# Pooling attention, then a soft mixture of experts, on one core: phi loaded from another DMA queue

## The chip, the cores and the metric

The kernel runs on one core of one Trainium2 chip. The metric is the device time of one execution in microseconds. The time before is the median of three runs.

## The reference

Queries, keys and values have 8 batches, 8 heads, 576 positions and 64 dimensions. Keys and values are averaged over groups of 8 positions, which leaves 72 of them; each query attends to these 72. The result, 4608 tokens of 512, goes through a soft mixture of 8 experts with 4 slots each.

```python
k_p = k.reshape(B, H, Sp, pool, D).mean(axis=3)
v_p = v.reshape(B, H, Sp, pool, D).mean(axis=3)
scores = scale * np.matmul(q, k_p.transpose(0, 1, 3, 2))
attn = softmax(scores)                       # over the 72 pooled keys
x = np.matmul(attn, v_p)  ->  (4608, 512)
...
logits = x @ phi                             # 4608 x 32 slots
d = softmax of logits over the tokens
slot_input = d.T @ x                         # 32 x 512
h = np.maximum(slot_input[e] @ w1[e], 0.0)   # per expert, 512 -> 1024
slot_out[e] = h @ w2[e]                      # 1024 -> 512
c = softmax of logits over the slots
out = c @ slot_out
```

The array in question is phi: 512 x 32 in fp32, 64 KB. The inputs q, k and v are 9.4 MB each, w1 and w2 16.8 MB each, the output is 9.4 MB.

## The kernel before

**Stages.** The batches are worked on in four pairs. For each pair the kernel loads keys, queries and values as bf16 (the DMA casts them from fp32), pools keys and values with matmuls against a pooling matrix (`pool_stage`, L232 and L236), turns means and queries (L248, L264), computes scores (L309), exponentials on ScalarE (L311), and the products with the pooled values (L331), which VectorE divides by their sums (L336, L342). The preparation of the next pair and the reduction over tokens of the previous pair are interleaved with the current pair by generators. After the fourth pair come the experts: the first layer (`hidden`), the second (`second_layer`, L585), and the products with the tokens (L642, L662, L665), whose results are scaled on VectorE and ScalarE (L621, L619) and stored.

**What phi is for.** The values are extended by 32 columns, so that the attention's product gives the logits along with x. For that, pooled values are multiplied by the matrix `iphi` (L294), which holds an identity and phi's part of each head. `iphi` is made once, near the start: VectorE multiplies phi by a selection of heads into `spread` (L179, four instructions, one for each j), four matmuls add it up into `phi_ps` (L184), and ScalarE copies the result into `iphi` (L188). These four matmuls stand at the head of TensorE's program, and two of them ahead of the first pooling matmul of pair 0.

**DMA queues.** Nearly all loads are issued by GpSimd (the page's POOL) on the software queue, in the order of the program: the second part of the first keys (L120), the queries (L100), phi (L131), the values and the keys of pair 1 (L100). SyncE (SP) issues the first 2048 columns of the first keys as fp32 on its hardware queue (L119); VectorE and ScalarE cast them (L149, L150). At the end SyncE issues all stores (L637). ScalarE (ACT) issues no DMA; its first instructions are the load of the activation table and a one-element exponential (both L138).

**What sets the order of loads.** `big` has four buffers, each for one load of q, k or v. The next load into a buffer is issued when the matmuls that read the old contents are through: `after_k`, `after_q` and `after_v` stand behind the last reading matmul of their stage. So the queries of pair 1 are issued behind the first pooling (L236), the values of pair 1 behind the turning of the queries (L264), and so on. w1 goes into its own place between these loads; w2 goes into buffers that the attention has left, the last of it in eight pieces (L533), of which each waits for the last use of its place or for the landing of an earlier DMA.

**Order of instructions.** In the first part the order on GpSimd is the program's (`manual_schedule`), and on the other engines a scheduler chooses it; behind the attention the program's order holds on all engines. With the change, the order on TensorE, VectorE and SyncE is as before; ScalarE has one DMA more, ahead of its table load, and GpSimd one less.

Of the kernel before, what the change touches and what calls it, by code (L numbers as in the profile page):

```python
# [8 lines left out]
FP = mybir.dt.float32  # L9
# [9 lines left out]
def kernel(  # L19
# [10 lines left out]
    nc = tc.nc  # L30

    B, H, S, D = q.shape
    POOL = 8
    SP = S // POOL
    DM = H * D
    E = moe_w1.shape[0]
    F = moe_w1.shape[2]
    NS = moe_phi.shape[1]
# [24 lines left out]
    consts = ctx.enter_context(tc.tile_pool(name="consts", bufs=1))  # L63
# [20 lines left out]
    def pair_of(src, pair):  # L84
        return src[2 * pair:2 * pair + 2].rearrange("b h (i t) d -> (b h i) (t d)", t=NT)
# [10 lines left out]
    def load(src, pair):  # L96
        nonlocal loaded
        loaded += 1
        t = big[:, loaded % 4]
        nc.gpsimd.dma_start(out=t, in_=pair_of(src, pair))  # L100
        return t.rearrange("p (t d) -> p t d", d=D)
# [12 lines left out]
                            in_=moe_w2[e:e + n].rearrange("e (p j) d -> p e j d", j=FJ)[:, :, j0:j1].rearrange("p e j d -> p e (j d)"))  # L114


    CUT = 4 * POOL * D
    kf = exf[:, 0:CUT]
    nc.sync.dma_start(out=kf, in_=pair_of(k, 0)[:, 0:CUT])  # L119
    nc.gpsimd.dma_start(out=big[:, 0, CUT:KQ], in_=pair_of(k, 0)[:, CUT:KQ])  # L120
    q_sb, k_sb, v_sb = {}, {}, {}
# [3 lines left out]
    nc.vector.memset(hT, 0.0)  # L125
    ident = consts.tile([128, 128], BF)
    make_identity(nc, ident)
    J = DM // 128
    A = D // J
    phi_f = consts.tile([128, J, NS], FP)  # L130
    nc.gpsimd.dma_start(out=phi_f, in_=moe_phi.rearrange("(p j) e -> p j e", j=J))  # L131
    v_sb[0] = load(v, 0)
    k_sb[1] = load(k, 1)

# [13 lines left out]

    nc.vector.tensor_copy(out=big[:, 0, 0:CUT // 2], in_=kf[:, 0:CUT // 2])  # L149
    nc.scalar.copy(out=big[:, 0, CUT // 2:CUT], in_=kf[:, CUT // 2:CUT])  # L150


    PAD = SP // 32 * 32
    nc.vector.memset(exf[PAD:128, CUT:], 0.0)
    nc.vector.memset(exf[PAD:128, 0:CUT], 0.0)
# [8 lines left out]
    with tc.tile_pool(name="tmp", bufs=1) as tmp:  # L164
        col = tmp.tile([128, A], FP, name="col")
        nc.vector.reduce_sum(out=col, in_=ident.rearrange("p (h a) -> p a h", a=A), axis=AX.X)
        head = tmp.tile([128, H], FP, name="head")
        nc.vector.reduce_sum(out=head, in_=ident.rearrange("p (h a) -> p h a", a=A), axis=AX.X)
        sel = tmp.tile([128, J, 2, A, J], BF, name="sel")
        nc.vector.memset(sel, 0.0)  # L170
        for j in range(J):
            nc.vector.tensor_copy(out=sel[:, j, :, :, j], in_=col.rearrange("p a -> p () a").to_broadcast([128, 2, A]))
        for r in range(2):
            rows = slice(r * D, (r + 1) * D)
            nc.vector.tensor_copy(out=iphi[rows, :, r, 0:D],
                                  in_=ident[rows, rows].rearrange("p d -> p () d").to_broadcast([D, HQ, D]))
        spread = tmp.tile([128, J, H, NS], BF, name="spread")
        for j in range(J):
# [350 lines left out]
    for half, cols in enumerate(halves):  # L529
        for e, j0, j1 in PIECES:  # L530
# [3 lines left out]
                                in_=moe_w2[e].rearrange("(p j) d -> p j d", j=FJ)[:, j0:j1, cols])  # L534
# [217 lines left out]
```

## Time and profile before

| | |
|---|---|
| median of three runs | 174.12 us (174.1 to 174.18) |
| the profiled execution | 174.13 us |
| its span, first to last instruction | 172.3 us |
| mean granted clock of TensorE | 0.973 |
| PE busy | 131.0 us (76%) |
| DVE busy | 100.6 us (58%) |
| ACT busy | 88.1 us (51%) |
| POOL busy | 27.5 us (16%) |
| HBM read and written | 61.93 MB and 9.44 MB |

Times in the profile are from the start of the span. PE is TensorE's matmul part and PEld its loading of weights, DVE is VectorE, ACT ScalarE, POOL GpSimd, SP SyncE; a "q" behind the name is the engine's sequencer. A row of an engine says start, length, line, operation, what is written and read, and in brackets how long the engine sat idle before it and what ended that. q0 is the software queue that GpSimd feeds, q1 the hardware queues. The DMA share is the mean over 16 DMA engines of the time that their packets took, put down to the moment at which a packet starts, so that it can come out above 1 in a short stretch. The rate in GB/s counts what is written: a load that casts to bf16 reads twice as much.

### The profile page before, as it was taken

What the parts mean: (1) busy time and instruction counts of PE and PEld (TensorE: products, weight loads), DVE (VectorE), ACT (ScalarE), POOL (GpSimd) and SP (SyncE); (2) the same over time, 40 slices, a digit from 0 to 9 for tenths busy, and PEclk for the clock granted to TensorE, in tenths of its full rate; (3) what the DMA queues carried; (4) which work ended last, traced back from release to release, by engine and by line L of the source; (5) the groups of instructions that cost most, each with busy time, mean ns of one, the idle gap of its engine ahead of it and who ended that gap; (6) DMA issues with size and microseconds to landing.
All of it is one profiled execution on the core that took longest, in us unless ns stands there. A gap on an engine that the chain in (4) does not pass through costs nothing.

```text
span 172.3 us, 2868 instructions
## 1 busy us (share of the span) xinstructions
PE 131.0 (76%) x1106; PEld 70.1 (41%) x1106; DVE 100.6 (58%) x265; ACT 88.1 (51%) x168; POOL 27.5 (16%) x42
## 2 busy tenths in 40 slices
PE   0005778899999999999789999887899998799100
PEld 0002353565555655556345554462442235343000
DVE  6686263478779658887975868750650102599300
ACT  3201337977686937988503998555021004799100
POOL 7000111022101032207001471120501030000000
PEclk9999999999999999999999999999999999999955
DMA  5999999999999999999999999999999999999994
GB/s 184 252 218 225 210 216 220 215 216 214 214 216 220 209 224 208 220 218 216 215 213 215 217 213 221 215 219 219 215 215 215 206 196 195 322 369 436 479 426 213
DMA packets 10589, 41.13 MB, mean 239 GB/s; under 512 B 704, under 2 KB 6592, under 8 KB 6864
## 3 DMA queue, kind: packets, MB, share of 16 engines
q0 software_dynamic: 7248, 30.48, 87.1%
q1 hardware_dynamic: 3328, 10.49, 15.5%
q8 instruction: 8, 0.13, 0.3%
q14 instruction: 5, 0.04, 0.1%
HBM read 61.93 MB, written 9.44 MB: 414 GB/s over the span
## 4 chain that ended last, share of the span: by engine, by line
PE 33%; DMA 28%; DVE 15%; ACT 12%; issue 3%; POOL 1%; DVEq 0%; POOLq 0%; ACTq 0%
DMA xsa<-in_moe_w_dram 21%; PE pool_ps L232 10%; DMA phi_f<-in_moe_phi_dram 7%; ACT exa L311 7%; DVE xsa L342 6%; PE u_ps L331 5%; PE sc L309 5%; PE q_ps L264 4%; DVE w_sb L621 4%; PE G_ps L366 3%; PE turn_ps L248 2%; ACT vmeans L238 2%; DVE rsum L240 2%; ACT vp L296 2%; DVE rec L336 2%
## 5 line engine op out<-in xcount | busy, mean ns | idle before, releaser
L311 ACT ACTIVATE exa<-sc 72x576 bf16<-72x576 f32 x64 | 39.3, 653 | 4.6 <-PE sc L309 3.8
L342 DVE TENSOR_TENSOR xsa<-u_ps,rec 128x384 bf16<-128x384 f32 x69 | 37.8, 554 | 1.7
L331 PE MATMUL u_ps<-vp,exa 128*128 128x97 bf16 (+5 forms) x320 | 31.3, 229 | 3.6 <-DVE xsa L342 3.0
L331 PEld LDWEIGHTS <-exa 128*128 128x128 bf16 (+1 forms) x320 | 18.9, 100 | 15.7 <-DVE xsa L342 6.5
L309 PE MATMUL sc<-qTa,kp 64*72 64x288 bf16 x128 | 20.5, 303 | 1.7 <-ACT exa L311 1.3
L232 PE MATMUL pool_ps<-big,pmat 128*128 128x512 bf16 x64 | 18.2, 411 | 0.7 <-ACT qTa L268 0.6
L336 DVE RECIPROCAL rec<-u_ps 128x4 f32<-128x4 f32 x72 | 11.9, 175 | 10.8 <-PE u_ps L331 10.5
L184 PE MATMUL phi_ps<-spread,sel 128*128 128x256 bf16 x4 | 1.3, 396 | 15.0 <-DVE spread L179 15.0
L268 ACT COPY qTa<-q_ps 128x768 bf16<-128x768 bf16 x8 | 6.3, 794 | 12.3 <-PE q_ps L264 12.3
L621 DVE TENSOR_SCALAR w_sb<-f_ps,recR 128x512 f32<-128x512 f32 (+1 forms) x19 | 11.3, 660 | 1.5 <-DMA xsa<-in_moe_w_dram 0.7
L264 PE MATMUL q_ps<-ident,big 128*128 128x128 bf16 x144 | 11.6, 219 | 0.8 <-DVE qTa L270 0.3
L309 PEld LDWEIGHTS <-kp 64*72 64x72 bf16 x128 | 7.7, 106 | 8.9 <-issue 3.5
L240 DVE TENSOR_REDUCE rsum<-rest_ps 128x64 f32<-128x512 f32 x8 | 5.5, 692 | 10.0 <-PE rest_ps L236 9.9
L642 PE MATMUL f_ps<-so,cT 128*128 128x512 bf16 (+1 forms) x38 | 10.1, 361 | 1.6 <-DVE so L621 0.9
L619 ACT ACTIVATE w_sb<-f_ps,recR 128x512 f32<-128x512 f32 (+1 forms) x19 | 10.3, 620 | 1.3 <-PE f_ps L642 1.1
L270 DVE COPY qTa<-q_ps 128x768 bf16<-128x768 bf16 x16 | 8.7, 551 | 2.3 <-PE q_ps L264 2.2
L264 PEld LDWEIGHTS <-big 128*128 128x128 bf16 x144 | 8.7, 97 | 3.0 <-issue 1.4
L533 POOL DMA_DIRECT2D xsa<-in_moe_w_dram x8 | 5.9, 744 | 23.2 <-DMA qTa<-in_moe_w_dram 8.9
L366 PE MATMUL G_ps<-xsa,ee 128*128 128x512 bf16 x36 | 8.4, 379 | 1.2 <-ACT ee L361 1.2
L232 PEld LDWEIGHTS <-pmat 128*128 128x128 bf16 x64 | 6.0, 103 | 6.8 <-issue 2.3
L619 ACT ACTIVATE so_a<-so_ps,recC 128x256 bf16<-128x256 f32 x2 | 0.9, 474 | 13.8 <-PE so_ps L585 13.8
L238 ACT CAST vmeans<-pool_ps 128x1024 bf16<-128x1024 f32 x4 | 4.0, 1012 | 6.8 <-PE pool_ps L232 6.8
(109 smaller groups left out, 166.8 us busy)
## 6 DMA issues: line engine op xcount, KB each, us to landing
w_sb<-in_moe_w_dram POOLq DMA_DIRECT2D x2, 3072.0 KB, 37.6
big<-in_q_dram POOLq DMA_DIRECT2D x4, 1152.0 KB, 12.7
big<-in_v_dram POOLq DMA_DIRECT2D x4, 1152.0 KB, 16.5
big<-in_moe_w_dram POOLq DMA_DIRECT2D x1, 4096.0 KB, 34.2
out_dram<-w_sb SPq DMA_DIRECT2D x1, 3584.0 KB, 10.2
big<-in_k_dram POOLq DMA_DIRECT2D x3, 1152.0 KB, 21.3
w_sb<-in_moe_w_dram POOLq DMA_DIRECT2D x2, 1024.0 KB, 19.2
qTa<-in_moe_w_dram POOLq DMA_DIRECT2D x1, 2048.0 KB, 30.9
```

What stands on the lines that cost most here:

```text
L232: nc.tensor.matmul(out=ps, lhsT=pmat, rhs=src[:, t:full * POOL:POOL, :], start=(t == 0), stop=(t == POOL - 1))
L240: nc.vector.reduce_sum(out=rsum, in_=rest.rearrange("p t d -> p d t"), axis=AX.X)
L264: nc.tensor.transpose(out=ps[:, t].rearrange("p n i -> p (n i)"), in_=q_sb[pair][:, tt:tt + 2, :].rearrange("p t d -> p (t d)"), identity= ...
L309: nc.tensor.matmul(out=ps[:, r, 0:S // 2], lhsT=kp[pair][rows, n], rhs=qT[pair][rows, n].rearrange("p t i -> p (t i)"), start=True, stop=True)
L311: nc.scalar.activation(out=dst.rearrange("p r (i t) -> p r i t", t=NU), in_=ps[:, :, 0:S // 2].rearrange("p r (t i) -> p r i t", i=NI), fu ...
L331: nc.tensor.matmul(out=bank[rows, hh * UW:(hh + times) * UW].rearrange("p (a c) -> p a c", a=times), lhsT=ex[b][:, hh].rearrange("p r t -> ...
L336: nc.vector.reciprocal(out=rec, in_=ps[:, :, XW])
L342: nc.vector.tensor_tensor(out=dst, in0=ps[:, :, 0:XW], in1=rec.rearrange("p h -> p h ()").to_broadcast([128, HQ, XW]), op=ALU.mult)
L366: nc.tensor.matmul(out=ps, lhsT=ee[:, t].rearrange("p g s -> p (g s)"), rhs=x[:, t, :, 0:D], start=(t == 0), stop=(t == 8))
L619: nc.scalar.activation(out=dst, in_=src, func=AF.Copy, scale=by)
L621: nc.vector.tensor_scalar(out=dst, in0=src, scalar1=by, scalar2=None, op0=ALU.mult)
L642: nc.tensor.matmul(out=bank[:, 0:times * (cols.stop - cols.start)].rearrange("p (a c) -> p a c", a=times), lhsT=tokens(n), rhs=rhs.rearran ...
```

## The change

The load of phi moves from GpSimd's software queue to ScalarE's hardware queue, and ahead of every other DMA in the program.

```diff
+    J = DM // 128
+    A = D // J
+    phi_f = consts.tile([128, J, NS], FP)
+    nc.scalar.dma_start(out=phi_f, in_=moe_phi.rearrange("(p j) e -> p j e", j=J))
+
+
     CUT = 4 * POOL * D
     kf = exf[:, 0:CUT]
     nc.sync.dma_start(out=kf, in_=pair_of(k, 0)[:, 0:CUT])
...
     nc.vector.memset(hT, 0.0)
     ident = consts.tile([128, 128], BF)
     make_identity(nc, ident)
-    J = DM // 128
-    A = D // J
-    phi_f = consts.tile([128, J, NS], FP)
-    nc.gpsimd.dma_start(out=phi_f, in_=moe_phi.rearrange("(p j) e -> p j e", j=J))
     v_sb[0] = load(v, 0)
     k_sb[1] = load(k, 1)
```

The lines behind it stand two higher in the changed kernel (L100 to L113 keep their numbers, L179 becomes L181, and so on).

## The prediction

> **What bounds the kernel now.** I read the page first, then the stretches by busy time, then the chain in order of time, then the DMA queues by stretch. The page says that the 16 DMA engines are busy in every slice but the first and the last:
>
> ```profile
> DMA  5999999999999999999999999999999999999994
> ...
> q0 software_dynamic: 7248, 30.48, 87.1%
> q1 hardware_dynamic: 3328, 10.49, 15.5%
> ```
>
> Slice digits hide short gaps, so here are the stretches (after the times: busy time of PE, PEld, DVE, ACT and POOL, granted clock, DMA share, GB/s written):
>
> ```profile
> 0.00:1.70 1.70, 0.00 (x0) 0.00 (x0) 0.68 (x1) 0.97 (x1) 0.67 (x5) 1.00 0.00 0
> 1.70:5.40 3.70, 0.00 (x0) 0.00 (x0) 2.52 (x4) 0.52 (x2) 2.82 (x7) 1.00 0.98 314
> 5.40:148.70 143.30, 121.23 (x1065) 65.51 (x1065) 86.44 (x243) 76.03 (x146) 24.02 (x31) 1.00 1.06 216
> 148.70:161.20 12.50, 9.79 (x43) 4.54 (x41) 10.99 (x19) 10.61 (x20) 0.00 (x0) 1.00 1.05 399
> 161.20:171.10 9.90, 0.00 (x0) 0.00 (x0) 0.00 (x0) 0.00 (x0) 0.00 (x0) 0.59 0.96 410
> ```
>
> Nothing moves before 1.70 us; from there to 171.1 the share is about 1. PE is busy 121.23 of 143.30 us, less than the DMA engines. The loads turn fp32 into bf16, so 216 GB/s written are about 432 GB/s read.
>
> The chain that ended last runs through phi at its start and through the w2 loads at its end:
>
> ```profile
> 2.98 11.52 DMA phi_f<-in_moe_phi_dram
> 14.53 0.44 DVE spread L179
> ...
> 111.47 28.52 DMA xsa<-in_moe_w_dram
> 140.03 0.48 issue
> 140.53 8.18 DMA xsa<-in_moe_w_dram
> 148.76 0.61 PE f_ps L662 x4
> ```
>
> This is the view to read with care. The chain holds 11.52 us of phi, but most of its middle is compute, and then comes one DMA of 28.52 us. That one is not long, it is queued: an earlier issue of it would only wait longer. Whether the middle matters depends on whether the software queue ever ran dry. These are its loads (start, length):
>
> ```profile
> 1.23 0.67 POOL L120 DMA_DIRECT2D big<-in_k_dram  x1 [0.79 <-POOLq L736]
> ...
> 2.98 0.56 POOL L131 DMA_DIRECT2D phi_f<-in_moe_phi_dram  x1
> 3.53 0.54 POOL L100 DMA_DIRECT2D big<-in_v_dram  x1
> 4.05 0.55 POOL L100 DMA_DIRECT2D big<-in_k_dram  x1
> 20.20 0.53 POOL L100 DMA_DIRECT2D big<-in_q_dram  x1 [15.60 <-PE rest_ps L236]
> 25.39 0.53 POOL L100 DMA_DIRECT2D big<-in_v_dram  x1 [4.66 <-PE q_ps L264]
> ```
>
> and their times to landing (KB, us), for the k of pair 1 issued at 4.05 and the q of pair 1 issued at 20.20:
>
> ```profile
> big<-in_k_dram POOLq DMA_DIRECT2D x1, 1152.0 KB, 21.3
> ...
> big<-in_q_dram POOLq DMA_DIRECT2D x1, 1152.0 KB, 10.7
> ```
>
> The k of pair 1 lands at 4.05 + 21.3 = 25.4, so q of pair 1, issued at 20.20, stands in the queue 5.2 us before its turn. It lands at 30.9, and the next v is issued at 25.39, 5.5 us ahead. With the share of 1.06 up to 148.70 this says: the queue stays full, and the end is set by the DMA work from 1.70 us on, then by the last w2 piece (140.53 + 8.18 = 148.71; PE starts on it at 148.76) and a tail behind it. **The kernel is bound by its DMA engines**, not by the compute chain that phi releases.
>
> **The change, part by part.**
>
> *The compute front.* DVE makes `spread` from phi. Before it DVE is in order:
>
> ```profile
> 13.47 0.22 DVE L175 COPY iphi<-ident 64x256 bf16<-64x256 bf16 x1
> 14.53 1.43 DVE L179 TENSOR_TENSOR spread<-phi_f,head 128x256 bf16<-128x256 f32 x4 [0.84 <-DMA phi_f<-in_moe_phi_dram]
> ```
>
> DVE is through at 13.69 and idles 0.84 us for phi. With phi some 8 us earlier, only these 0.84 us can go: next late is DVE's own row of memsets and copies. `spread`, phi_ps, the first pooling and so the issue at 20.20 come up to 0.84 us earlier. I count it as nothing at the end, since that load then queues 6.0 us instead of 5.2. If the cover were gone it would be worth 0.84 us.
>
> *POOL's issue goes.* v of pair 0 and k of pair 1 are issued 0.56 us earlier, behind at least 5 us of queued loads: nothing.
>
> *phi leaves the software queue.* 65.5 KB, read without a cast, at the 432 GB/s worked out above are 0.15 us of all 16 engines. Everything behind phi, down to the last w2 piece, comes 0.15 us earlier: **-0.15**.
>
> *phi joins the hardware traffic at the start.* It competes there with the first keys, and it is not free, since the engines are busy as soon as they move anything:
>
> ```profile
> 1.00:2.00 1.00, 0.00 (x0) 0.00 (x0) 0.95 (x2) 1.00 (x1) 0.77 (x2) 1.00 0.64 106
> 2.00:3.00 1.00, 0.00 (x0) 0.00 (x0) 0.44 (x1) 0.22 (x2) 0.93 (x4) 1.00 0.56 164
> ...
> 4.00:5.00 1.00, 0.00 (x0) 0.00 (x0) 0.81 (x2) 0.00 (x0) 0.60 (x2) 1.00 1.06 405
> ```
>
> Up to 4.5 us only the hardware queue moves; in the next microsecond the software queue takes over, and its first load, issued at 1.23, lands 7.6 us later, at 8.8 (answers for 0 to 4.5 and for 4.5 to 5.5; packets, MB, share):
>
> ```profile
> q1 hardware_dynamic: 108, 0.88, 59.6%
> ...
> big<-in_k_dram POOLq DMA_DIRECT2D x1, 640.0 KB, 7.6
> ```
> ```profile
> q0 software_dynamic: 27, 0.14, 68.4%
> q1 hardware_dynamic: 36, 0.16, 39.5%
> ```
>
> So the software stream starts when the hardware packets are through, and what phi takes there pushes all of the stream back. Its price isn't in the trace; I bound it. Below: nothing at all, hidden in the slow first packets (106 and 164 GB/s where 405 come later). Middle: 128 rows of 512 B as packets of their own. The nearest small hardware packets are the output rows of 1 KB:
>
> ```profile
> q1 hardware_dynamic: 142, 0.14, 39.8%
> ```
>
> (147 to 148 us): 0.398 x 1 us x 16 / 142 = 45 ns each. Eight of them an engine are 0.36 us; at half the size, if time goes with bytes, 0.18. Above: phi pays a start of its own like the keys. They need 1.70 to 5.40, 3.7 us, where 1.05 MB at 405 GB/s are 2.6: 1.1 us lost. I take **+0.25**, between 0.18 and 0.36, as these are rows of the same queue kind.
>
> *ACT.* The issue stands ahead of the table load, and of dummy and the cast of the first keys:
>
> ```profile
> 0.73 1.28 ACT L138 ACT_TABLE_LOAD   x1 [0.73 <-PEq L736]
> 0.74 0.37 SPq L119 DMA_DIRECT2D exa<-in_k_dram  x1
> ...
> 5.81 1.04 ACT L150 CAST big<-exa 128x1024 bf16<-128x1024 f32 x1 [3.58 <-DMA exa<-in_k_dram]
> ```
>
> An issue on SP's queue takes 0.37 us; 3.58 us of idle time hide it. If the keys land 0.25 us later, both casts and DVE's row behind them slip as much: the front's gain falls from 0.84 to about 0.6, still hidden. SP's order is untouched.
>
> Sum against the profiled run's own 174.13 us (its span is 172.3, the rest lies outside; the median of the runs is 174.12): 0 + 0 - 0.15 + 0.25 + 0 = +0.10. **Forecast: 174.2 us**, no difference; its own bounds are -0.15 and +0.2.
>
> A rule speaks against the change: the Trainium skill, "DMA: Bandwidth & Descriptors", section "Issuing engines are not separate DMA queues", says that DMAs of all issuing engines run on the same 16 engines, and that another issuer only saves the sequencer's issue time. By it phi's bytes cost the same on either queue, and the sum would be 0 in place of +0.10; the trace's full DMA share is in line with it.
>
> **The rivals.**
>
> *The front is the bound.* Then 0.84 us go: 174.13 - 0.84 = 173.3. For it: the chain's 11.52 us of phi. Against it: 5.2 us of queue at 20.20 and the share of 1.06. It decides if a load is ever issued into an empty queue. 0.10.
>
> *A second start-up.* On the other side: phi's packets go into the stretch where the engines run at 106 to 164 GB/s, and delay each engine's keys by more than their bytes, up to the 1.1 us above. The software stream starts behind the slowest engine, and the end moves as much: +0.35 to +1.1 - 0.15, so 174.5 to 175.1. It decides when phi holds an engine for over 0.5 us (0.15 + 0.35). For it: half of the keys' time at the start is such loss. Against: the bytes are a sixteenth of the keys'. 0.26.
>
> *phi falls behind the software queue*, so that the change does the contrary of what it says. If an engine takes k, q, v and k in the software ring before it looks at ACT's, phi lands near 25.4 in place of 14.5, POOL's issue slips by those 10.9 us from 20.20 to 31.1, and the engines stand idle from 25.4 on: 174.13 + 5.7 = about 180. For it: one queue was served after the other at the start. Against: phi is issued near 0.73, ahead of POOL's first load at 1.23. 0.04. The same page, section "Queues, rings and completion order", says that each engine goes round the queues that have work, packet by packet; by that phi could not be kept waiting, and this rival would have no chance. The takeover after 4.5 us doesn't show such turns, unless the software ring was ready only then, which no row here tells.
>
> **How the numbers follow.** About 0.2% (0.35 us) is what a measurement of this kernel can tell from no change: 173.78 to 174.48. Forecast 0.60, within it; the front 0.10, faster; the second start 0.26 and the queue 0.04, slower. So faster 0.10, same 0.60, slower 0.30. The range takes in the forecast and the second start: 173.8 to 175.1 leaves out the front and the queue, 0.14, and little of the forecast.
>
> **What would show it.** Right: phi lands near 6 us; no wait of DVE for it at `spread`, which starts at 13.7 to 14.0; the load after the first pooling is issued at 19.4 to 19.9; the DMA share stays at 1.0; the last w2 piece lands within 0.3 us of 148.71. First failing step to look for: the takeover by the software queue. If it comes over 0.5 us later than 4.5 to 5.5, the second start holds. If the end comes 0.8 us earlier although the share is unchanged, the front was the bound. If phi lands after 20 us, the queue rival holds. Wrong would also be a last w2 piece that moves otherwise than the first software load: then something between them, not phi, decides.

## The result and the profile after

The changed kernel takes 174.59 us (median of nine runs, 174.53 to 174.75), the kernel before 174.13 us in the same comparison. The medians lie 0.46 us apart. The ratio is 1.0024, with a 95% interval of 1.0015 to 1.0033: slower by some 0.4 us, just past the 0.2% that had been called the limit of no change.

First the page of the changed kernel, the rows that answer to those shown of before. q10 is new: ScalarE's hardware queue.

```profile
DMA  5999999999999999999999999999999999999994
...
q0 software_dynamic: 7216, 30.41, 86.8%
q1 hardware_dynamic: 3328, 10.49, 15.4%
...
q10 hardware_dynamic: 144, 0.07, 0.1%
```

Then the stretches of the changed kernel, cut at the same places (busy PE, PEld, DVE, ACT, POOL, granted clock, DMA share, GB/s):

```profile
0.00:1.70 1.70, 0.00 (x0) 0.00 (x0) 0.68 (x1) 0.54 (x1) 0.67 (x5) 1.00 0.00 0
1.70:5.40 3.70, 0.00 (x0) 0.00 (x0) 2.52 (x4) 0.95 (x2) 2.29 (x6) 1.00 0.95 320
5.40:148.70 143.30, 121.20 (x1065) 65.41 (x1065) 86.36 (x243) 76.02 (x146) 24.02 (x31) 1.00 1.06 215
148.70:161.20 12.50, 9.88 (x44) 4.54 (x41) 11.05 (x19) 10.61 (x20) 0.00 (x0) 1.00 1.03 391
161.20:171.10 9.90, 0.00 (x0) 0.00 (x0) 0.00 (x0) 0.00 (x0) 0.00 (x0) 0.56 0.99 424
171.10:172.80 1.70, 0.00 (x0) 0.00 (x0) 0.00 (x0) 0.00 (x0) 0.00 (x0) 0.50 0.00 0
```

Up to 171.1 us nothing has changed that would be worth half a microsecond: the shares and rates are about the same. But the last stretch, in which no engine computes and no DMA moves, is 1.70 us long; before it ran from 171.10 to 172.3, 1.2 us. The loss stands there, behind all the work.

The front did what the prediction said. DVE's timeline of the changed kernel (start, length) shows `spread` without a wait for phi, at 13.83 in place of 14.53, and GpSimd's shows the load behind the first pooling at 19.50 in place of 20.20:

```profile
13.57 0.22 DVE L177 COPY iphi<-ident 64x256 bf16<-64x256 bf16 x1
13.83 1.43 DVE L181 TENSOR_TENSOR spread<-phi_f,head 128x256 bf16<-128x256 f32 x4
```
```profile
19.50 0.53 POOL L100 DMA_DIRECT2D big<-in_q_dram  x1 [15.44 <-PE rest_ps L238]
```

And the far end of the load stream, TensorE's first matmul on the last piece of w2 in the changed kernel, which stood at 148.76:

```profile
148.81 0.61 PE f_ps L664 x4
```

So 0.70 us gained at the front are gone at 148.8 us, where the kernel is 0.05 us late. From there to the end of the span another 0.4 us are lost. To see them, look at what SyncE does behind the last store. L747 (L749 in the changed kernel) is the end of the program: SyncE checks there, one after the other, the semaphores that tell of landed DMAs and of the other engines' last work. First its waits behind the last store's issue (us in total, times, longest), before and after:

```profile
SPq L747 <- DMA out_dram<-w_sb: 9.4, 2, 8.4
SPq L747 <- PEq L747: 0.7, 2, 0.5
```
```profile
SPq L749 <- DMA out_dram<-w_sb: 9.8, 1, 9.8
SPq L749 <- PEq L749: 0.7, 2, 0.5
```

Before, SyncE waited twice, for the last two stores, each when its turn came. After, it meets the last store early in its list and waits for it in one piece. What it does once that store has landed (count, ns min/median/max, first and last start), before and after:

```profile
L747 SPq EVENT_SEMAPHORE  x3: 17/17/28, 171.4 to 172.3; - x3
L747 SPq DRAIN  x3: 7/7/7, 171.5 to 171.8; - x3
```
```profile
L749 SPq EVENT_SEMAPHORE  x10: 17/28/28, 171.5 to 172.7; - x10
L749 SPq DRAIN  x3: 7/7/7, 172.0 to 172.3; - x3
```

Two of these, before and after, belong to the meeting of all engines at the very end. The others are checks: one before, eight after, and the first DRAIN follows 0.1 us or 0.5 us behind the landing. Taken alone, the eight start between 171.5 and 171.9:

```profile
L749 SPq EVENT_SEMAPHORE  x8: 28/28/28, 171.5 to 171.9; - x8
```

Seven steps in about 0.4 us are some 0.06 us for each check. What the seven others wait for had happened long before, and still each takes its turn. The last store itself lands 0.07 us later than before; together that is the difference of the spans, 172.3 and 172.8 us.

Why is the order another one? A DMA tells of its landing through a completion semaphore, a counter that it raises. In the built programs the hardware DMAs take eight of these in turn, in the order of the program (DMAHW0 to DMAHW7; the DMASW ones belong to the software queue). The last store's row in the built program shows which one it has: a DMA that takes a semaphore again waits for that semaphore's earlier user.

```
before
16 L637 DMACopy out_dram<-w_sb 128x7168 [waits DMASW0_49,DMAHW7_49,DVE_49,Activation_49]
changed
16 L639 DMACopy out_dram<-w_sb 128x7168 [waits DMASW7_49,DMAHW0_49,DVE_49,Activation_49]
```

Before there are 16 hardware DMAs (the first keys and 15 stores), and the last store falls on number 7, the last of the list. phi is a seventeenth, placed first: every store moves one on, and the last one falls on number 0, near the head of the list. That is the theory to be tested, the **wait-list theory**. Its rivals: the **start theory** (phi's packets beside the first keys delay the load stream, and the end with it, which is the prediction's second start-up), and the **queue theory** (the use of a second hardware queue costs something at the end).

### The profile page after: what moved, and what is told of

Read it like the earlier page. It is cut to its first block, busy times and chain, and to the rows that moved or that the text cites. A ratio compares the mean times of both kernels' runs of the same rounds, so it can differ in the third digit from the quotient of the medians.

```text
span 172.8 us, 2869 instructions
## 1 busy us (share of the span) xinstructions
PE 131.1 (76%) x1106; PEld 70.0 (40%) x1106; DVE 100.6 (58%) x265; ACT 88.1 (51%) x168; POOL 27.0 (16%) x41
## 4 chain that ended last, share of the span: by engine, by line
PE 32%; DMA 27%; DVE 18%; ACT 12%; issue 4%; DVEq 0%; POOLq 0%; ACTq 0%
DMA qTa<-in_moe_w_dram 18%; PE pool_ps L234 10%; ACT exa L313 7%; DMA xsa<-in_moe_w_dram 5%; PE sc L311 5%; DVE xsa L344 4%; PE u_ps L333 4%; PE q_ps L266 4%; DVE w_sb L623 4%; DMA exa<-in_k_dram 3%; PE G_ps L368 2%; PE turn_ps L250 2%; ACT vmeans L240 2%; DVE rsum L242 2%; ACT vp L298 2%
```

## The experiments

Each comparison below has its own runs of the kernel before on the same chip: 174.15 us for the first four, 174.16 us for the others.

**One tiny load more, phi left alone.** Added to the kernel before, behind the first loads:

```diff
+    junk = consts.tile([16, 1, NS], FP)
+    for i in range(1):
+        nc.sync.dma_start(out=junk[:, i], in_=moe_phi[16 * i:16 * i + 16])
```

> Phi stays on the software queue; one tiny load (2 KB of phi into a tile that nothing reads) is added on SyncE's queue at the start, so that the hardware queues carry 17 DMAs and the last store falls on the first of the eight completion semaphores, as in the changed kernel. Wait-list theory (SyncE checks the semaphores one after the other at the end, and what stands behind the last store's costs 61 ns each): 7 x 0.061 = +0.43, 174.55 us, with some 0.9 + 0.43 = 1.3 us from the last landing to the end of the span. Start theory (phi's packets at the start delay the load stream): 2 KB are nothing, 174.13. Queue theory (opening ScalarE's queue costs at the end): that queue stays shut, 174.13.

Measured: 174.63 us, ratio 1.0028 (1.0018 to 1.0038). The checks of this kernel behind the last landing:

```profile
L751 SPq EVENT_SEMAPHORE  x10: 17/28/28, 171.5 to 172.8; - x10
L751 SPq DRAIN  x3: 7/7/7, 172.0 to 172.3; - x3
```

The whole loss is there with phi on its old queue and nothing on ScalarE's. The start theory and the queue theory both gave 174.13.

**Four tiny loads.** The same edit with 4 in place of 1.

> As before with four tiny loads of 2 KB on SyncE's queue at the start: 20 hardware DMAs, the last store falls on the fourth semaphore. Wait-list theory: four checks behind it, 4 x 0.061 = +0.24, 174.37 us. Start theory and queue theory: 174.13, or up to 0.1 more if four small DMAs disturb the start.

Measured: 174.46 us, ratio 1.0017 (1.0008 to 1.0025). Seven semaphore instructions of SyncE are left behind the last landing, that is five checks:

```profile
L751 SPq EVENT_SEMAPHORE  x7: 17/28/28, 171.6 to 172.7; - x7
```

More DMAs than with one, and faster: the number of DMAs isn't the price, the place of the last one is.

**Eight tiny loads.** The same edit with 8.

> As before with eight tiny loads of 2 KB on SyncE's queue at the start: 24 hardware DMAs, the last store falls on the eighth semaphore again. Wait-list theory: 174.13 us, although this one has the most added DMAs. A theory by which each further hardware DMA costs something at the start or at the end: the most of the three, 174.5 or more.

Measured: 174.33 us, ratio 1.0014 (1.0005 to 1.0022). The list is down to where it was:

```profile
L751 SPq EVENT_SEMAPHORE  x3: 17/17/28, 171.6 to 172.4; - x3
```

So the 0.4 us of the list are gone again, but 0.18 us stay that the wait-list theory alone doesn't give; with one and four loads, 0.06 and 0.07 us are left above what 7 and 4 more checks of 0.06 us give. The tiny loads do disturb something a little. The traces show where: ahead of the last piece of w2. TensorE starts on it at 148.76 us before, and with one, four and eight loads at 148.86, 149.00 and 148.88 (timeline with eight):

```profile
148.88 0.50 PE L666 MATMUL f_ps<-xsa,zT 128*128 128x256 bf16 x3
```

These profiled executions took 174.62, 174.54 and 174.22 us, so the delay at this point needn't be that of the median run. What the tiny loads do to the load stream wasn't followed up.

**The changed kernel with one store less.** phi stays first on ScalarE's queue; two stores of one row become one of two rows, which makes 16 hardware DMAs:

```diff
-    begin(0, ((0, 1), (1, 2), (2, 4)))
+    begin(0, ((0, 2), (2, 4)))
```

> The changed kernel with the first two stores of one row each merged into one of two rows: 16 hardware DMAs, the last store is on the eighth semaphore again, phi is still the first DMA of ScalarE's queue. Wait-list theory: the end costs 0.9 us again, and only the 0.07 us by which the last store landed later are left: 174.2 us. Start theory: 174.59, since phi's packets are where they were. Queue theory: 174.59, since ScalarE's queue is still used.

Measured: 174.14 us, ratio 1.0000 (0.9991 to 1.0009). The list behind the last landing:

```profile
L749 SPq EVENT_SEMAPHORE  x3: 17/17/28, 171.5 to 172.3; - x3
```

This is the run that decides: ScalarE's queue and phi's packets are where they were, and the loss is gone. The start theory and the queue theory gave 174.59.

**The same merged store in the kernel before**, to see that the merge isn't a gain of its own. The edit is the one above, on the kernel before.

> The kernel before with the same merged store: 15 hardware DMAs, the last store falls on the seventh semaphore, so one check stands behind it. Wait-list theory, if the merge itself does nothing: 174.15 + 0.06 = 174.21 us. If merging the two stores were itself worth the 0.4 us that the merged variant of the changed kernel gained, this one would come to 173.7 + 0.06.

Measured: 174.22 us, ratio 1.0001 (0.9992 to 1.0010). The median lies where one check more puts it (0.06), though the interval alone couldn't tell that from nothing; the list shows it:

```profile
L747 SPq EVENT_SEMAPHORE  x4: 17/22/28, 171.5 to 172.4; - x4
```

The merge is not worth 0.4 us.

**phi on SyncE's queue**, behind the first keys, with the merged store (the edit is on the changed kernel):

```diff
-    nc.scalar.dma_start(out=phi_f, in_=moe_phi.rearrange("(p j) e -> p j e", j=J))
...
     nc.sync.dma_start(out=kf, in_=pair_of(k, 0)[:, 0:CUT])
+    nc.sync.dma_start(out=phi_f, in_=moe_phi.rearrange("(p j) e -> p j e", j=J))
```

> Phi on SyncE's queue behind the first keys, ScalarE issues nothing, stores merged as above: 16 hardware DMAs, the last store on the eighth semaphore. Wait-list theory: 174.15 us, as phi's 64 KB cost the stream the same on either queue (within 0.1). Queue theory or start theory (a second queue beside the keys is what costs): no change against the merged variant with ScalarE's queue either, if that one already shows nothing; a difference of over 0.15 us between the two would be the price of the second queue.

Measured: 174.11 us, ratio 0.9999 (0.9990 to 1.0008). That is 0.03 us from the variant with ScalarE's queue: no price of a second queue is to be seen, within the 0.15 us that had been set for it.

**No load of phi**, in the kernel before:

```diff
-    nc.gpsimd.dma_start(out=phi_f, in_=moe_phi.rearrange("(p j) e -> p j e", j=J))
+    nc.vector.memset(phi_f, 0.0)
```

> Phi isn't loaded: VectorE fills its tile with zeros, so the logits are zero and the output is that of phi = 0. 16 hardware DMAs as before. This is the term of what phi costs in the software stream by itself: -0.15 us by the prediction's bytes, 174.0. If the compute front that waits for phi were the bound, 0.7 to 0.84 less: 173.3 to 173.45.

Measured: 174.01 us, ratio 0.9991 (0.9982 to 1.0000). In its trace the load behind the first pooling is as early as in the changed kernel, and the last piece of w2 comes 0.07 us earlier than before (timelines of GpSimd and TensorE):

```profile
19.51 0.53 POOL L100 DMA_DIRECT2D big<-in_q_dram  x1 [15.44 <-PE rest_ps L236]
```
```profile
148.69 0.61 PE L662 MATMUL f_ps<-xsa,zT 128*128 128x256 bf16 x4
```

The front comes 0.69 us earlier, the end 0.15 us by the medians: the front is not the bound. The 0.15 us are what the prediction's sum gave for phi's bytes, but they are small against what can be told apart: the interval reaches from 0 to 0.3 us, and the trace shows 0.07.

**phi twice.** phi on the software queue as before, and a copy into an unused tile on ScalarE's queue, with the merged store (the edit is on the changed kernel):

```diff
-    nc.scalar.dma_start(out=phi_f, in_=moe_phi.rearrange("(p j) e -> p j e", j=J))
+    phi_h = consts.tile([128, J, NS], FP)
+    nc.scalar.dma_start(out=phi_h, in_=moe_phi.rearrange("(p j) e -> p j e", j=J))
...
+    nc.gpsimd.dma_start(out=phi_f, in_=moe_phi.rearrange("(p j) e -> p j e", j=J))
     v_sb[0] = load(v, 0)
```

> Phi stays on the software queue, and a second copy comes on ScalarE's queue at the start into a tile that nothing reads; stores merged, so 16 hardware DMAs and the eighth semaphore. This is the term of what phi costs beside the first keys by itself: +0.25 us by the prediction (174.4), about +0.12 by the later end of the hardware packets on the slowest engine in the changed kernel (174.27), 0.35 or more by a second start-up (174.5 and above).

Measured: 174.31 us, ratio 1.0011 (1.0002 to 1.0019). The last piece of w2 is 0.24 us late:

```profile
149.00 0.39 PE L666 MATMUL f_ps<-xsa,zT 128*128 128x256 bf16 x2
```

By the runs' medians phi beside the first keys costs 0.15 us, as much as in the software stream; the interval reaches from 0.03 to 0.33 us.

## Why the prediction was right and wrong

The measured 174.59 us lies inside the range of 173.8 to 175.1, but the forecast of 174.2 is 0.4 us off, and the case behind it, no change, failed by a little (its limit was 174.48). That the range holds the time is luck: its upper part was there for a second start-up, which isn't what made the kernel slower. Step by step:

**The bound: right.** The changed kernel's front is 0.70 us earlier and the run without phi's load 0.69 us, and neither end followed by as much. The rival "the front is the bound", worked out from the chain's 11.52 us of phi, is refuted: a chain says what came last at each step, not what the time would be without it.

**phi out of the software queue, -0.15: borne out as far as the runs can tell.** The run without the load gives 0.15 us by the medians, 0 to 0.3 by the interval.

**phi into the hardware queues, +0.25: perhaps too high.** The run with two copies gives 0.15 us by the medians, 0.24 us at the last piece of w2 in its trace, and the interval of 0.03 to 0.33 us holds both. The estimate went between 45 ns, a packet of 1 KB of the output, and half of that. The changed kernel's packets up to 4.5 us show what one of phi's took (packets, MB, share of 4.5 us on 16 engines):

```profile
q1 hardware_dynamic: 98, 0.80, 52.7%
q10 hardware_dynamic: 83, 0.04, 3.2%
```

0.032 x 4.5 us x 16 / 83 = 28 ns each, 0.22 us for the eight of an engine. A part of that may hide in the slow start of the keys; no run shows how much. The two terms about cancel: the two variants with 16 hardware DMAs are at 1.0000 and 0.9999, each within 0.16 us. Here the rule of the Trainium skill that the prediction set against the change, "DMA: Bandwidth & Descriptors", section "Issuing engines are not separate DMA queues", came out closer by the medians than the prediction's own sum: it gave 0 for these two terms, the sum +0.10, and the intervals hold both.

**ACT's issue: right.** The table load moved back, and the cast of the first keys waited for the keys as before, 0.11 us later than at 5.81:

```profile
1.16 1.28 ACT L140 ACT_TABLE_LOAD   x1 [1.16 <-PEq L738]
...
5.92 1.04 ACT L152 CAST big<-exa 128x1024 bf16<-128x1024 f32 x1 [3.25 <-DMA exa<-in_k_dram]
```

**"SP's order is untouched": the step that failed.** It was true of SyncE's instructions and false of their semaphores. The sum counted what phi's DMA does at its issue, its packets and its landing, and not that the DMA takes a completion semaphore and so renumbers those of all later stores on another engine. The term that was missing, 7 checks of some 0.06 us, is 0.42 us, nearly the whole measured loss of 0.46 us. It could have been seen ahead: the waits of the built program show the new numbers, and the trace of before shows SyncE's wait of 8.4 us for the last store as the last of its list.

**The rival "a second start-up": right in size, wrong in cause.** Its 174.5 to 175.1 hold the measured time. Its case was made too strong: 1.1 of the keys' 3.7 us are less than a third, not half. Its mark is nearly there: the software queue's first packet moves before 4.7 us in the kernel before, and only behind 5.1 us in the changed one, where the mark was half a microsecond. From 4.5 to 5.5 us it has 15 packets in place of 27.

```profile
q1 hardware_dynamic: 44, 0.25, 59.0%
q0 software_dynamic: 15, 0.08, 37.3%
q10 hardware_dynamic: 57, 0.02, 8.0%
```
```profile
big<-in_k_dram POOLq DMA_DIRECT2D x1, 640.0 KB, 7.7
```

But the first software load lands hardly later, 7.7 us behind its issue in place of 7.6, and the changed kernel with one store less has nearly the same start (no software packet before 4.9 us, and in the same stretches as above) without the loss:

```profile
q0 software_dynamic: 16, 0.08, 39.8%
```
```profile
big<-in_k_dram POOLq DMA_DIRECT2D x1, 640.0 KB, 7.8
```

A rival that names the right time isn't shown by that.

**The rival "phi falls behind the software queue": refuted.** phi lands 5.3 us after its issue.

```profile
phi_f<-in_moe_phi_dram ACTq DMA_DIRECT2D x1, 64.0 KB, 5.3
```

The packets above show the two hardware queues served side by side, 98 packets against 83 up to 4.5 us. That is in line with the rule of the Trainium skill, "DMA: Bandwidth & Descriptors", section "Queues, rings and completion order", that each engine takes turns between its queues packet by packet; the turns of a single engine are not shown here. Why the software queue starts only when the hardware packets are nearly through stays open.

No variant beats the kernel before: the best of those that do all of the work, phi on SyncE's queue with the merged store, is at 0.9999 (0.9990 to 1.0008).

## What to carry to other kernels

When a DMA is added or moved between queues, look also at what it shifts by being counted: here one more hardware DMA moved the last store's semaphore from the end of the final list of checks to near its head, and that cost more than all that the transfer itself did. Compare the idle stretch behind the last landing before and after, and choose the number of DMAs so that the one that lands last is checked last. With the DMA engines busy throughout, as here, the 0.7 us gained at the compute front bought nothing, and moving bytes to another queue saved nothing that could be measured.

## What the runs showed of the hardware

A check of semaphores that have long been reached isn't free: about 0.06 us of SyncE for each EVENT_SEMAPHORE instruction, seen with 1, 2, 5 and 8 of them behind the last landing. A hardware packet of 512 B took 28 ns at the start of the changed kernel, against 45 ns for the 1 KB packets of the output in the kernel before.
